# A spectral filter and a gated causal convolution on one core: filter loaded in fp32 through ScalarE's queue and converted on chip, sine tables with fewer passes and ordered ahead of what waits for the filter

## The chip, the core and the metric

The kernel runs on one core of a Trainium2 chip. The engines are PE (TensorE, matmuls; PEld is its weight load), DVE (VectorE), ACT (ScalarE), POOL (GpSimd) and SP (SyncE, which only issues DMAs here). Sixteen DMA engines move data between the chip's memory and the core's SBUF. The metric is the device time of one execution in microseconds (us), lower is better. The kernel before took 385.33 us, the median of 3 runs (384.27 to 386.5).

## What is computed

```python
def _attn_ref(x, filt_r, filt_i):            # x: (8, 3200, 256), filters: (1601, 256)
    X = np.fft.rfft(x, axis=1)
    F = (filt_r + 1j * filt_i)[None, :, :]
    return np.fft.irfft(X * F, n=x.shape[1], axis=1)

def _moe_ref(x, w_val, conv_w, w_out):       # x is the result above
    xp = np.concatenate([np.zeros((B, K - 1, D)), x], axis=1)      # K = 5
    for k in range(K):
        gate_pre += conv_w[k] * xp[:, k:k + S, :]
    gate = 1.0 / (1.0 + np.exp(-gate_pre))
    return gate * (x @ w_val) @ w_out
```
All inputs and the output are fp32. Each of the 8 batches has 3,200 positions of 256 channels.

## The kernel before

A Fourier transform of length 3,200 is done as two stages of small transforms, 3,200 = 128 x 25, each a matmul with a table of sines and cosines in fp16. A batch goes through these steps, each cut into seven chunks:

- `load_x` (L86, POOL's queue): x from memory, converted from fp32 to bf16 on the way. `xin` has 10 buffers, so three chunks of the next batch have room before the first seven are used.
- `s1` (first stage): PE multiplies with the matrix `cf_t` (L307), DVE evicts PSUM to the tile `so` (L310), and SP writes `so` to the scratch `dscr` in memory (L312). There are four PSUM tiles and four `so` buffers.
- `load_t` (SP): after all seven chunks are written, the scratch is read back in another order into the tiles `tt` (L326 to L329).
- `s2` (second stage): PE multiplies with `wc_t`, `ws_t`, `wsn_t` (L340 to L346), ACT evicts to `xs` (L349), and DVE multiplies with the filter: `za` with its real half `fr_t` (L354), `zb` with its signed imaginary half `fm_t` (L358), and their sum `z` (L360).
- `inva`: the inverse with `vc_t`, `vs_t`, `vsn_t` (L376, L378), evicted by ACT to `u` (L381) and written to the scratch `escr` (L392); `load_v` reads it back (L398).
- `invb` (L413 to L422), `conv` (L431, matrices `dg_t`, then the sigmoid on ACT), `val` (L448, L453), `outp` (L465 to L475): last inverse stage, causal convolution, gate and output.

A loop over 81 steps G runs all of these with lags: `s1` of chunk t at step t, `s2` at t + 9, `inva` at t + 10, `invb` at t + 19, `conv` at t + 21, `outp` at t + 23. So several batches are under way at once.

Before the loop stands a set-up, which the change is about. It builds the tables on the chip. An index product is made from iotas of POOL (`pcol`, `kc`, `kv`, `kt`, `nv`), reduced modulo the period by `floormod`, seven passes of DVE over the array (L103 to L113), and turned into a sine by ACT (L134, L182, L188). `expand` then spreads 25 columns of a group over five blocks with a mask `mk`, one multiply for each of 13 groups (L171), and `negate` makes the third table (L177). `sincos` does this for the `w` tables and again for the `v` tables. The filter is read by 24 DMAs on POOL's queue (L216 to L225) straight into bf16 tiles: twelve for each half, most of them 13 rows of 13 pieces or 12 rows of 13. DVE multiplies the imaginary half with a sign in each row, twice (L232, L234). Then come `ci_t` (L267) and the convolution's matrices `dg_t` (L284), twenty scalings on DVE.

A framework lays out each engine's instruction order: from text order as priority and from its own estimate of when things are ready. So the order on an engine is not the text's: `dg_t`, near the end of the set-up, has instructions among the first table passes. It also sets all waits, and the memory of the set-up's pools (`gen`, `gen2`, `genf`) is used again by pools opened after them. Each engine takes its instructions in the order laid out; issuing a DMA is an instruction of the engine that owns the queue.

## Time and profile before

| what | value | how to read it |
|---|---|---|
| median of 3 runs | 385.33 us | the time that is compared |
| the profiled execution | 387.95 us | one execution, the one that the profile shows |
| its span | 385.9 us | from the first to the last recorded instruction |
| PE / DVE / ACT / POOL busy | 312.3 / 284.9 / 229.1 / 64.2 us | whole span |
| DVE busy, 10 to 20 us | 9.97 us | the set-up's tables |
| hardware queue q1 | 78.98 MB, 62.5% | bytes, share of 16 engines' span |
| software queue q0 (POOL's) | 15.04 MB, 28.1% | the same; counted at bf16 |
| x loads 256 KB, issue to landing | 6.5 us | median over the run |
| half-filter pieces 78 KB, issue to landing | 6.2 us (real), 3.9 us (imaginary) | medians |

In the views, a row of the timeline has the start, the duration, engine, line, operation and tiles, and in brackets how long the engine sat idle before it and what it waited for. Busy shares count no instruction that only issues a DMA, save POOL's.

### The profile page before, as it was taken

What the parts mean: (1) busy time and instruction counts of PE and PEld (TensorE: products, weight loads), DVE (VectorE), ACT (ScalarE), POOL (GpSimd) and SP (SyncE); (2) the same over time, 40 slices, a digit from 0 to 9 for tenths busy, and PEclk for the clock granted to TensorE, in tenths of its full rate; (3) what the DMA queues carried; (4) which work ended last, traced back from release to release, by engine and by line L of the source; (5) the groups of instructions that cost most, each with busy time, mean ns of one, the idle gap of its engine ahead of it and who ended that gap; (6) DMA issues with size and microseconds to landing.
All of it is one profiled execution on the core that took longest, in us unless ns stands there. A gap on an engine that the chain in (4) does not pass through costs nothing.

```text
span 385.9 us, 8019 instructions
## 1 busy us (share of the span) xinstructions
PE 312.3 (81%) x3089; PEld 206.9 (54%) x3089; DVE 284.9 (74%) x462; ACT 229.1 (59%) x255; POOL 64.2 (17%) x131
## 2 busy tenths in 40 slices
PE   0230477475899999999997999899999999999992
PEld 0100145253656756766675666566676677666661
DVE  4999958553858887888787789678977677765554
ACT  1100235334976777677765776677677878867660
POOL 8797211112110211021102011100010001001000
PEclk9999998766989999999999999999999999999998
DMA  7999999999999999999999999989595968449343
GB/s 124 144 162 190 216 257 251 231 250 280 179 250 249 311 286 273 263 282 332 274 301 303 286 269 298 285 299 319 201 351 170 304 223 299 136 142 323 141 191 152
DMA packets 94118, 94.53 MB, mean 245 GB/s; under 512 B 10102, under 2 KB 74624, under 8 KB 94080
## 3 DMA queue, kind: packets, MB, share of 16 engines
q1 hardware_dynamic: 80064, 78.98, 62.5%
q0 software_dynamic: 14016, 15.04, 28.1%
q8 instruction: 24, 0.39, 0.4%
q14 instruction: 14, 0.11, 0.1%
HBM read 56.59 MB, written 52.43 MB: 282 GB/s over the span
## 4 chain that ended last, share of the span: by engine, by line
PE 44%; DVE 20%; DMA 19%; SPq 8%; issue 4%; ACT 2%; POOL 1%; DVEq 0%; ACTq 0%; POOLq 0%
PE ps L431 12%; PE ps L448 7%; DMA escr<-u 6%; PE ps L465 6%; DVE so L310 6%; DMA vt<-escr 5%; SPq L326 5%; PE ps L413 5%; DMA dscr<-so 4%; PE ps L376 3%; DVE gv L453 3%; DMA tt<-dscr 3%; PE ps L378 3%; PE ps L307 3%; DVE za L354 2%
## 5 line engine op out<-in xcount | busy, mean ns | idle before, releaser
L415 ACT ACTIVATE yt<-ps 128x1024 bf16<-128x1024 f32 (+1 forms) x56 | 52.1, 931 | 44.3 <-PE ps L413 44.2
L453 DVE TENSOR_TENSOR gv<-ps,gt 128x1024 bf16<-128x1024 f32 (+1 forms) x56 | 61.9, 1104 | 18.7 <-PE ps L448 13.7
L310 DVE CAST so<-ps 128x1024 bf16<-128x1024 f32 (+1 forms) x56 | 61.5, 1103 | 19.0 <-PE ps L307 15.9
L354 DVE TENSOR_TENSOR za<-xs,fr_t 125x1024 bf16<-125x1024 bf16 (+1 forms) x56 | 37.3, 665 | 50.5 <-ACT xs L349 50.3
L381 ACT ACTIVATE u<-ps 125x1024 bf16<-125x1024 f32 (+1 forms) x56 | 53.9, 963 | 24.4 <-PE ps L378 21.6
L431 PE MATMUL ps<-yt,dg_t 64*64 64x512 bf16 (+1 forms) x1120 | 65.7, 361 | 0.8
L349 ACT ACTIVATE xs<-ps 125x1024 bf16<-125x1024 f32 (+1 forms) x56 | 54.0, 965 | 19.6 <-PE ps L346 18.4
L436 ACT ACTIVATE gt<-ps 128x1024 bf16<-128x1024 f32 (+1 forms) x56 | 52.4, 935 | 9.1 <-PE ps L431 5.9
L86 POOL DMA_DIRECT2D xt<-in_x_dram x56 | 30.2, 569 | 153.0 <-PE ps L307 146.5
L307 PE MATMUL ps<-xt,cf_t 128*128 128x512 bf16 x112 | 36.9, 421 | 22.4 <-DVE so L310 11.4
L465 PE MATMUL ps<-wo_t,gv 128*128 128x256 bf16 x400 | 52.8, 273 | 0.9 <-DVE gv L453 0.9
L448 PE MATMUL ps<-yt,wv_t 128*128 128x512 bf16 (+1 forms) x224 | 52.6, 357 | 0.0
L465 PEld LDWEIGHTS <-gv 128*128 128x128 bf16 x400 | 39.1, 98 | 14.9 <-DVE gv L453 1.2
L413 PE MATMUL ps<-ci_t,vt 128*128 128x128 f16 x400 | 31.9, 221 | 13.3 <-DMA vt<-escr 9.6
L431 PEld LDWEIGHTS <-dg_t 64*64 64x64 bf16 x1120 | 30.1, 106 | 23.2 <-issue 10.1
L340 PE MATMUL ps<-tt,wc_t 125*128 125x256 bf16 x104 | 30.1, 289 | 12.9 <-DMA tt<-dscr 10.6
L470 DVE COPY o<-ps 128x1024 f32<-128x1024 f32 (+1 forms) x32 | 36.7, 1148 | 1.1 <-PE ps L465 1.1
L360 DVE TENSOR_TENSOR z<-za,zb 125x1024 bf16<-125x1024 bf16 (+1 forms) x56 | 36.4, 650 | 1.3
L413 PEld LDWEIGHTS <-vt 128*128 128x128 bf16 x400 | 27.0, 98 | 17.9 <-DMA vt<-escr 10.7
L358 DVE TENSOR_TENSOR zb<-xs,fm_t 125x1024 bf16<-125x1024 bf16 (+1 forms) x56 | 36.2, 646 | 0.0
L376 PE MATMUL ps<-z,vc_t 125*128 125x256 bf16 x104 | 30.0, 289 | 6.9 <-DVE z L360 6.9
L307 PEld LDWEIGHTS <-cf_t 128*128 128x128 f16 x112 | 9.2, 108 | 41.7 <-issue 28.2
(109 smaller groups left out, 386.6 us busy)
## 6 DMA issues: line engine op xcount, KB each, us to landing
out_dram<-o SPq DMA_DIRECT2D x32, 512.0 KB
tt<-dscr SPq DMA_DIRECT2D x48, 256.0 KB
escr<-u SPq DMA_DIRECT2D x48, 224.0 KB
out_dram<-o SPq DMA_DIRECT2D x24, 384.0 KB
xt<-in_x_dram POOLq DMA_DIRECT2D x32, 256.0 KB, 6.5
dscr<-so SPq DMA_DIRECT2D x32, 256.0 KB
vt<-escr SPq DMA_DIRECT2D x32, 256.0 KB
xt<-in_x_dram POOLq DMA_DIRECT2D x24, 192.0 KB, 5.7
```

Source lines behind the costliest of these rows:

```text
L307: nc.tensor.matmul(ps[:, a * D:e * D], lhsT=cf_t[:, 0:128], rhs=xt[:, a:e, :], start=True, stop=True)
L310: nc.vector.tensor_copy(so[:, 0:np_, :].rearrange("p a d -> p (a d)"), ps[:, 0:np_ * D])
L349: nc.scalar.activation(xs[0:P2, 0:ng, :, :].rearrange("p g c d -> p (g c d)"), ps[0:P2, 0:ng * 512], AF.Copy)
L354: nc.vector.tensor_tensor(za[0:P2, 0:ng], xs[0:P2, 0:ng], fr_t[0:P2, g0:g0 + ng, :].unsqueeze(2).to_broadcast((P2, ng, 2, D)), op=ALU.mult)
L381: nc.scalar.activation(u[0:P2, 0:2 * ng, :].rearrange("p q d -> p (q d)"), ps[0:P2, 0:ng * 512], AF.Copy)
L413: nc.tensor.matmul(ps[:, o:o + L], lhsT=v[:, a, 128 * dh:128 * dh + 128], rhs=ci_t[:, :], start=True, stop=True)
L415: nc.scalar.activation(y[:, :, H + p0:H + p0 + np_, :].rearrange("p h a n -> p h (a n)"), ps[:, :].rearrange("p (h n) -> p h n", h=2)[:, : ...
L431: nc.tensor.matmul(ps[64 * dh:64 * dh + 64, 512 * r:512 * r + np_ * L], lhsT=dg_t[rows, dh, k, :], rhs=y[rows, dh, p0 + k:p0 + k + np_, :] ...
L436: nc.scalar.activation(g[:, :, 0:np_ * L], ps[:, :].rearrange("p (h n) -> p h n", h=2)[:, :, 0:np_ * L], AF.Sigmoid)
L448: nc.tensor.matmul(ps[:, 512 * eh:512 * eh + np_ * L], lhsT=wv_t[:, dh, 128 * eh:128 * eh + 128], rhs=y[:, dh, H + p0:H + p0 + np_, :], st ...
L453: nc.vector.tensor_tensor(gv[:, :, 0:np_ * L], ps[:, :].rearrange("p (h n) -> p h n", h=2)[:, :, 0:np_ * L], g[:, :, 0:np_ * L], op=ALU.mult)
L465: nc.tensor.matmul(ps[:, D * a:D * a + D], lhsT=gv[:, eh, L * a:L * a + L], rhs=wo_t[:, eh, :], start=(eh == 0), stop=(eh == 1))
```

## The change

`s1` and `load_t` are defined ahead of the set-up, and batch 0's seven `s1` stand in the text right after `cf_t`; ACT instead of DVE evicts chunks 1, 3 and 5 of batch 0. The iotas `pcol` and `kc` come after the first x load instead of after the seventh. `floormod` is replaced: the product is scaled to turns, a large constant is added and taken away to round it, the rounded value is subtracted, and ACT takes the sine of the rest (three passes, one scaling ahead of them). `expand` becomes one multiply over all groups; `negate`, the two `fm_t` scalings and `dg_t` go to ACT. The filter is read in fp32 into `ff` by the same 24 pieces on ACT's queue, the real half's after ACT's eviction of chunk 1 and the imaginary half's after that of chunk 3 (`issue_after` lays them out behind the instruction named). DVE converts the real half after the last `v` table; ACT converts and signs the imaginary half. `zpool` and `upool` are opened before the set-up's pools. The small arrays `lp` and `rp` get new formulas, which the diff leaves out, as it does the unchanged parts of moved functions.

```diff
--- before.py
+++ after.py
@@ -65,13 +65,14 @@
     dg_t = cpool.tile([128, 2, K, 64], BF16, name="dg_t")
     wv_t = cpool.tile([128, 2, D], BF16, name="wv_t")
     wo_t = cpool.tile([128, 2, D], BF16, name="wo_t")
-    b_npi = cpool.tile([128, 1], FP32, name="b_npi")
 
     pp = ctx.enter_context(tc.tile_pool(name="ps", bufs=4, space=bass.MemoryType.PSUM))
     dpool = ctx.enter_context(tc.tile_pool(name="scr", bufs=2, space=bass.MemoryType.DRAM))
     xpool = ctx.enter_context(tc.tile_pool(name="xin", bufs=10))
     spool = ctx.enter_context(tc.tile_pool(name="s1o", bufs=4))
     tpool = ctx.enter_context(tc.tile_pool(name="s2i", bufs=8))
+    upool = ctx.enter_context(tc.tile_pool(name="ivo", bufs=4))
+    zpool = ctx.enter_context(tc.tile_pool(name="zed", bufs=3))
 
     def psum():
         return pp.tile([128, 1024], FP32, name="ps", tag="ps")
@@ -86,53 +87,85 @@
         nc.gpsimd.dma_start(out=xt[:, 0:np_, :], in_=src)
         xts[(b, j)] = xt
 
-    for j in range(NCH):
+    def iota(pool, shape, pattern, base, cm, name):
+        t = pool.tile(shape, FP32, name=name)
+        nc.gpsimd.iota(t[...], pattern=pattern, base=base, channel_multiplier=cm,
+                       allow_small_or_imprecise_dtypes=True)
+        return t
+
+    load_x(0, 0)
+    pcol = iota(cpool, [128, 1], [[0, 1]], 0, 1, "pcol")
+    kc = iota(cpool, [128, NG, 2, GL], [[5, NG], [0, 2], [1, GL]], 1, 0, "kc")
+    for j in range(1, NCH):
         load_x(0, j)
+
+
+    st = {}
+
+    def s1(b, j):
+        if j == 0:
+            st[("D", b)] = dpool.tile([128 * R + 64, D], BF16, name="dscr")
+        dscr = st[("D", b)]
+        p0, np_ = PCH[j]
+        xt = xts.pop((b, j))
+        ps = psum()
+        for a in range(0, np_, 2):
+            e = min(a + 2, np_)
+            nc.tensor.matmul(ps[:, a * D:e * D], lhsT=cf_t[:, 0:128],
+                             rhs=xt[:, a:e, :], start=True, stop=True)
+        so = spool.tile([128, 4, D], BF16, name="so")
+        sov = so[:, 0:np_, :].rearrange("p a d -> p (a d)")
+        if b == 0 and j % 2 == 1:
+            st[("Sact", j)] = nc.scalar.activation(sov, ps[:, 0:np_ * D], AF.Copy)
+        else:
+            nc.vector.tensor_copy(sov, ps[:, 0:np_ * D])
+        nc.sync.dma_start(
+            out=dscr[0:128 * R, :].rearrange("(i r) d -> i r d", r=R)[:, p0:p0 + np_, :],
+            in_=so[:, 0:np_, :])
+
+    def load_t(b, j):
...
+        st[("T", b, j)] = t
 
 
     with tc.tile_pool(name="gen", bufs=1) as g1, \
          tc.tile_pool(name="gen2", bufs=2) as g2, \
          tc.tile_pool(name="genf", bufs=1) as gf:
 
-        def floormod(src_ap, divisor):
-            shp = list(src_ap.shape)
...
-            return q
-
-        def iota(shape, pattern, base, cm, name):
-            t = g1.tile(shape, FP32, name=name)
-            nc.gpsimd.iota(t[...], pattern=pattern, base=base, channel_multiplier=cm,
-                           allow_small_or_imprecise_dtypes=True)
-            return t
-
-        nc.vector.memset(b_npi[:, :], -PI)
-        pcol = iota([128, 1], [[0, 1]], 0, 1, "pcol")
-
-
-        kc = iota([128, NG, 2, GL], [[5, NG], [0, 2], [1, GL]], 1, 0, "kc")
+        MAGIC = 1.5 * 2.0 ** 23
+
+        def sine(dst, t):
+
+            r = g2.tile(list(t.shape), FP32, name=f"sr{t.shape[1]}")
+            nc.vector.tensor_scalar(r[...], t, MAGIC, None, op0=ALU.add)
+            nc.vector.tensor_scalar(r[...], r[...], -MAGIC, None, op0=ALU.add)
+            nc.vector.tensor_tensor(r[...], t, r[...], op=ALU.subtract)
+            nc.scalar.activation(dst, r[...], AF.Sin, scale=2.0 * PI * (1.0 - 2e-7))
+
+
         nc.vector.memset(kc[:, NG - 1, 0, GL - 1:GL], 0.0)
         pr = g1.tile([128, NG, 2, GL], FP32, name="pr")
-        nc.vector.tensor_scalar(pr[...], kc[...], pcol[:, 0:1], None, op0=ALU.mult)
-        nc.vector.tensor_scalar(pr[:, :, 0, :], pr[:, :, 0, :], 0.75 * L, None,
-                                op0=ALU.add)
-        q = floormod(pr[...].rearrange("p g c l -> p (g c l)"), L)
-        nc.scalar.activation(cf_t[:, :], q[...], AF.Sin, bias=b_npi[:, 0:1],
-                             scale=2.0 * PI / L)
+        nc.vector.tensor_scalar(pr[...], kc[...], pcol[:, 0:1], 1.0 / L, op0=ALU.mult,
+                                op1=ALU.mult)
+        for c in range(2):
+            nc.vector.tensor_scalar(pr[:, :, c, :], pr[:, :, c, :], 0.25 * (c + 1), None,
+                                    op0=ALU.add)
+        sine(cf_t[:, :], pr[...].rearrange("p g c l -> p (g c l)"))
+
+        for j in range(NCH):
+            s1(0, j)
 
         ident = g1.tile([128, 128], FP32, name="ident")
         nc.vector.memset(ident[:, :], 1.0)
...
@@ -165,31 +200,32 @@
                                 channel_multiplier=-1)
         nc.vector.tensor_copy(mk[...], mkf[...])
 
-        def expand(dst, src):
+        def expand(eng, dst, src):
             nc.gpsimd.memset(dst[:, :, P2:128], 0.0)
-            for g in range(NG):
-                nc.vector.tensor_tensor(
-                    dst[:, g, 0:P2].rearrange("p (l r) -> p l r", l=GL),
-                    src[:, g, :].unsqueeze(1).to_broadcast((128, GL, R)),
-                    mk[...], op=ALU.mult)
+            return eng.tensor_tensor(
+                dst[:, :, 0:P2].rearrange("p g (l r) -> p g l r", l=GL),
+                src[...].unsqueeze(2).to_broadcast((128, NG, GL, R)),
+                mk[...].unsqueeze(1).to_broadcast((128, NG, GL, R)), op=ALU.mult)
 
         def negate(dst, src):
-            nc.vector.tensor_scalar(dst[...], src[...], -1.0, None, op0=ALU.mult)
-
-        def sincos(prod, dc, ds, dsn):
-            qs = floormod(prod[...].rearrange("p g r -> p (g r)"), N)
+            nc.scalar.activation(dst[...].rearrange("p g m -> p (g m)"),
+                                 src[...].rearrange("p g m -> p (g m)"),
+                                 AF.Copy, scale=-1.0)
+
+        def sincos(eng, prod, dc, ds, dsn):
             sn = g2.tile([128, NG, R], FP16, name="sn")
-            nc.scalar.activation(sn[...].rearrange("p g r -> p (g r)"), qs[...],
-                                 AF.Sin, bias=b_npi[:, 0:1], scale=2.0 * PI / N)
+            cs = g2.tile([128, NG, R], FP16, name="cs")
             pc = g2.tile([128, NG, R], FP32, name="pc")
-            nc.vector.tensor_scalar(pc[...], prod[...], 0.75 * N, None, op0=ALU.add)
-            qc = floormod(pc[...].rearrange("p g r -> p (g r)"), N)
-            cs = g2.tile([128, NG, R], FP16, name="cs")
-            nc.scalar.activation(cs[...].rearrange("p g r -> p (g r)"), qc[...],
-                                 AF.Sin, bias=b_npi[:, 0:1], scale=2.0 * PI / N)
-            expand(dc, cs)
-            expand(dsn, sn)
-            negate(ds, dsn)
+            flat = prod[...].rearrange("p g r -> p (g r)")
+            pcf = pc[...].rearrange("p g r -> p (g r)")
+            nc.vector.tensor_scalar(pcf, flat, 1.0 / N, 0.25, op0=ALU.mult, op1=ALU.add)
+            sine(cs[...].rearrange("p g r -> p (g r)"), pcf)
+            expand(eng, dc, cs)
+            nc.vector.tensor_scalar(flat, flat, 1.0 / N, None, op0=ALU.mult)
+            sine(sn[...].rearrange("p g r -> p (g r)"), flat)
+            last = expand(eng, ds, sn)
+            negate(dsn, ds)
+            return last
 
         HK = R // 2 + 1
         kv = g1.tile([128, NG, R], FP32, name="kv")
@@ -202,40 +238,40 @@
         nc.vector.tensor_scalar(kv[:, NG - 1, :], kv[:, NG - 1, :], lw[:, 0:1], None,
                                 op0=ALU.add)
         nc.vector.tensor_scalar(kv[...], kv[...], rp[:, 0:1], None, op0=ALU.mult)
-        sincos(kv, wc_t, ws_t, wsn_t)
-
-
-        fi_t = gf.tile([128, NG, D], BF16, name="fi_t")
+        sincos(nc.vector, kv, wc_t, ws_t, wsn_t)
+
+        for j in range(NCH):
+            load_t(0, j)
+
+
+        ff = gf.tile([128, 2, NG, D], FP32, name="ff")
 
         def fsrc(f, row, ap):
             return bass.AP(tensor=f.tensor, offset=f.offset + row * D, ap=ap + [[1, D]])
 
-        for f, dst in ((filt_r, fr_t), (filt_i, fi_t)):
+        def load_f(f, c):
+            dst = ff[:, c]
             for l in range(GL):
                 ng = NG if l < GL - 1 else NG - 1
-                nc.gpsimd.dma_start(
+                nc.scalar.dma_start(
                     out=dst[R * l:R * l + HK, 0:ng, :],
                     in_=fsrc(f, l + 1, [[L * D, HK], [GL * D, ng]]))
-                nc.gpsimd.dma_start(
+                nc.scalar.dma_start(
                     out=dst[R * l + HK:R * (l + 1), 0:ng, :],
                     in_=fsrc(f, L - l - 1, [[L * D, HK - 1], [-GL * D, ng]]))
             lo = R * (GL - 1)
-            nc.gpsimd.dma_start(out=dst[lo:lo + HK, NG - 1, :],
+            nc.scalar.dma_start(out=dst[lo:lo + HK, NG - 1, :],
                                 in_=fsrc(f, 0, [[L * D, HK]]))
-            nc.gpsimd.dma_start(out=dst[lo + HK:lo + R, NG - 1, :],
+            nc.scalar.dma_start(out=dst[lo + HK:lo + R, NG - 1, :],
                                 in_=fsrc(f, L, [[L * D, HK - 1]]))
-        sg = g1.tile([128, 1], FP32, name="sg")
-        sgn = g1.tile([128, 1], FP32, name="sgn")
-        nc.vector.tensor_scalar(sg[...], rp[...], HK - 0.5, None, op0=ALU.is_lt)
-        nc.vector.tensor_scalar(sg[...], sg[...], 2.0, -1.0, op0=ALU.mult, op1=ALU.add)
-        nc.vector.tensor_scalar(sgn[...], sg[...], -1.0, None, op0=ALU.mult)
-        nc.vector.tensor_scalar(fm_t[0:P2, :, 0, :], fi_t[0:P2, :, :], sgn[0:P2, 0:1],
-                                None, op0=ALU.mult)
-        nc.vector.tensor_scalar(fm_t[0:P2, :, 1, :], fi_t[0:P2, :, :], sg[0:P2, 0:1],
-                                None, op0=ALU.mult)
-
-
-        kt = iota([128, NG], [[5, NG]], 1, 0, "kt")
+
+        with tc.issue_after(st[("Sact", 1)].ins):
+            load_f(filt_r, 0)
+        with tc.issue_after(st[("Sact", 3)].ins):
+            load_f(filt_i, 1)
+
+
+        kt = iota(g1, [128, NG], [[5, NG]], 1, 0, "kt")
         nc.vector.tensor_scalar(kt[...], kt[...], lp[:, 0:1], None, op0=ALU.add)
         nc.vector.tensor_scalar(kt[:, NG - 1:NG], kt[:, NG - 1:NG], lw[:, 0:1], None,
                                 op0=ALU.add)
@@ -248,11 +284,24 @@
         nc.vector.tensor_tensor(rl[...], rl[...], rp[...], op=ALU.add)
         nc.vector.tensor_scalar(rl[...], rl[...], float(L), None, op0=ALU.mult)
         nc.vector.tensor_scalar(kt[...], kt[...], rl[:, 0:1], None, op0=ALU.add)
-        nv = iota([128, NG, R], [[0, NG], [1, R]], 0, 0, "nv")
+        nv = iota(g1, [128, NG, R], [[0, NG], [1, R]], 0, 0, "nv")
         nc.vector.tensor_tensor(nv[...], nv[...],
                                 kt[...].unsqueeze(2).to_broadcast((128, NG, R)),
                                 op=ALU.mult)
-        sincos(nv, vc_t, vs_t, vsn_t)
+        vs_ins = sincos(nc.vector, nv, vc_t, vs_t, vsn_t)
+
+
+        sg = g1.tile([128, 1], FP32, name="sg")
+        sgn = g1.tile([128, 1], FP32, name="sgn")
+        nc.vector.tensor_scalar(sg[...], rp[...], HK - 0.5, None, op0=ALU.is_lt)
+        nc.vector.tensor_scalar(sg[...], sg[...], 2.0, -1.0, op0=ALU.mult, op1=ALU.add)
+        nc.vector.tensor_scalar(sgn[...], sg[...], -1.0, None, op0=ALU.mult)
+        with tc.issue_after(vs_ins.ins):
+            nc.vector.tensor_copy(fr_t[0:P2, :, :], ff[0:P2, 0])
+        nc.scalar.activation(fm_t[0:P2, :, 0, :], ff[0:P2, 1], AF.Copy,
+                             scale=sgn[0:P2, 0:1])
+        nc.scalar.activation(fm_t[0:P2, :, 1, :], ff[0:P2, 1], AF.Copy,
+                             scale=sg[0:P2, 0:1])
 
 
         ac = g1.tile([128, 1], FP32, name="ac")
@@ -281,53 +330,15 @@
                                     in_=moe_w_out[ch:ch + 64, :])
                 for k in range(K):
                     rows = slice(64 * r, 64 * r + 64)
-                    nc.vector.tensor_scalar(dg_t[rows, dh, k, :],
-                                            ident[rows, 64 * r:64 * r + 64],
-                                            cw[rows, dh, k:k + 1], None, op0=ALU.mult)
-
-    zpool = ctx.enter_context(tc.tile_pool(name="zed", bufs=3))
-    upool = ctx.enter_context(tc.tile_pool(name="ivo", bufs=4))
+                    nc.scalar.activation(dg_t[rows, dh, k, :],
+                                         ident[rows, 64 * r:64 * r + 64], AF.Copy,
+                                         scale=cw[rows, dh, k:k + 1])
+
     vpool = ctx.enter_context(tc.tile_pool(name="ivi", bufs=8))
     ypool = ctx.enter_context(tc.tile_pool(name="yout", bufs=2))
     gpool = ctx.enter_context(tc.tile_pool(name="gate", bufs=3))
     opool = ctx.enter_context(tc.tile_pool(name="ost", bufs=4))
 
...
 
     def s2(b, j):
         g0, ng = GCH[j]
@@ -502,7 +513,7 @@
         if c is not None:
             conv(*c)
         c = at(G, 0)
-        if c is not None:
+        if c is not None and c[0] > 0:
             s1(*c)
             if c[1] == NCH - 1:
                 for j in range(NCH):
```

## The prediction

> **What bounds the kernel now.** I read the table of slices first: PE is under half busy for the first ten slices and nearly full afterwards, while DVE is full early. So the start differs from the rest. Then the windows, which put numbers on it, and the chain of waits, which says why.
>
> ```profile
> PE   0230477475899999999997999899999999999992
> DVE  4999958553858887888787789678977677765554
> ...
> 0.00:45.00 45.00, 8.33 (x19) 2.13 (x19) 38.35 (x157) 3.96 (x6) 34.13 (x70) 1.00 1.09 164
> 45.00:92.70 47.70, 29.52 (x165) 19.21 (x166) 30.76 (x43) 18.29 (x19) 5.59 (x12) 0.83 1.05 244
> 92.70:386.00 293.30, 274.46 (x2906) 185.61 (x2906) 215.74 (x263) 206.89 (x230) 24.44 (x49) 0.98 0.86 258
> ```
> The windows' columns are window, sum, then busy us of PE, PEld, DVE, ACT, POOL, then clock, DMA share, GB/s. After 92.7 us PE works 274 of 293 us: that part has the same code after the change. Before it PE works 37.9 of 92.7 us. The change can win only there.
>
> ```profile
> 10.07 0.40 ACT L134 ACTIVATE cf_t<-fm_q,b_npi 128x130 f16<-128x130 f32 x1 [7.98 <-DVE fm_q L113]
> ...
> PE ps L307 <- DVE so L310: 11.4, 3, 10.8
> ...
> 22.87 1.24 DVE so L310
> ...
> 31.03 3.13 DMA dscr<-so
> 34.60 1.70 SPq L326
> 37.03 4.30 SPq L326
> 41.37 5.33 SPq L326
> 46.75 4.58 SPq L326
> ...
> 45.09 0.37 PE L340 MATMUL ps<-tt,wc_t 125*128 125x256 bf16 x1 [4.11 <-DMA tt<-dscr]
> ```
> The first-stage matrix is ready at 10.5, and PE fills its PSUM tiles by 13.4; then it waits 10.8 us for the first eviction, which stands behind the sine tables on DVE until 22.87. The seven evictions end at 31.0, the write to scratch lands at 34.2, and the loads back take until 52.8 to issue, because batch 1's x loads are on the way at once. The first second-stage matmul runs at 45.1, the first product z ends at 51.2 (50.52 + 0.68), the last z of batch 0 at 73.2, and the first inverse matmul (L413) starts at 92.7. The filter is not in this chain: its landed halves are scaled at 33.2 to 37.0 (L232, L234), 11 us before they are used.
>
> **The change, part by part.**
>
> *x and the first matrix.* Only one x load (0.55 us) stands ahead of the two iotas (0.21 + 0.66), so kc is there at 1.31 + 0.55 + 0.87 = 2.7 instead of 6.0. Ahead of the Sin remain pr 0.55, two adds 0.22 each, three sine passes (0.26 + 0.26, and 0.28 as the nearest two-operand row): 1.8 us. With Sin 0.40, cf_t is ready at about 5, not 10.5. x is then late: the last of batch 0 is issued at 5.2 + 0.9 = 6.1 and takes 6.8 us to land, 12.9.
>
> *Evictions ahead of the tables.* Four on DVE (1.22 or 0.95), three on ACT (0.93 as L381 averages); after the last x a matmul pair (0.85) and one eviction, so the last `so` ends at about 15 against 31.0, its write lands (3.1) at 18 against 34.2: 16 us. The loads back took 11 us from first issue to first use (34.2 to 45.1), so 29 here, if they meet the same company.
>
> *Tables.* floormod's seven passes were 0.32 + 0.32 + 0.48 + 0.32 + 0.49 + 0.32 + 0.49 = 2.7 us for 325 columns; now a scaling and three passes, 0.32 x 3 + 0.49 = 1.45. Four times 1.3 is 5 us less DVE. The mask multiplies (13 x 0.14 pitch, 1.8 us) become one of 1,625 columns: between 0.95 (the rate of za, 706 ns for 1,024) and 1.8; I take 1.7, since broadcast operands resemble the old rows. Two negations (0.58) leave DVE for ACT, where the two Sin shapes give 0.84 ns a column (404 ns for 130, 568 for 325) on 0.295: 1.7 us each. Twenty dg_t scalings move too: 0.35 us each, 7.0; they are first read by L431 at 106.9, which covers them unless they stand ahead of the second stage's evictions, where they would cost their 7.0. DVE's saving buys nothing by itself, since evictions no longer wait for it.
>
> *Filter.* This becomes late next. Its 24 issues leave POOL, where they stood from 7.69 to 25.6 (17.9 us, 15.0 of it issuing); so batch 1's x loads start at about 31.8 - 17.9 = 13.9 and will share the DMA engines with filter, scratch write and loads back. On ACT they come behind evictions of chunks 1 and 3. An issue costs 0.46 us by the escr rows (median): 11 us. Three evictions and two Sin add 4, so from 10 the last is out at about 25 undisturbed. Data: 1.66 MB becomes 3.33 MB fp32, and the hardware queue spent 62.5% of the span on 78.98 MB, 3.05 us per MB: 10.2 us. The software queue spent 28.1% on 15.04 MB, 7.2 us per MB: the halves cost 12 there. That is even. Landing: at best 26 (25 and little company); at worst behind ten x loads, the buffers there are, 2.3 MB at the 205 GB/s of 8 to 12 us = 11.4 us, and the scratch traffic (3.3 MB, 10 us), 43. I take 33, in the middle, as all three queues get turns (in 40 to 48 us x had 89% and the loads back 24% of the engines' time).
>
> By the Trainium skill ("DMA: Bandwidth & Descriptors", section "Why a DMA increments its semaphore by 16 and not by 1") a transfer issued from this kind of queue spreads over the largest number of engines up to 16 that divides its slowest dimension; these pieces have 13 or 12 rows. No row of this trace shows it. It speaks against the change: an estimate by it is 10.2 x 16 / 12.5 = 13 us, and the forecast below would be 3 us less gain. I stay with the row.
>
> *Conversion.* fm_t on ACT: 2 x (0.295 + 3,328 x 0.84 ns) = 6.2 us (at the 1.0 ns of L349, 6.8), against 3.9 on DVE. fr_t on DVE, 2.0 us, runs beside it. Had the filter still been early, this would be free; now it is on the path. Two new waits come with it: fm_t waits for the filter on ACT, with dg_t and the second stage's evictions (L349) behind it, and fr_t on DVE, with batch 1's evictions and za behind it; SP carries none of the filter, and its loads back pass it by. So fm_t is ready at 39.2, and zb and z (0.69 each) end at 40.6 to 41, against 51.2: **-10 us**.
>
> *From there.* Batch 0's z came every (73.2 - 51.2) / 6 = 3.67 us. With everything landed DVE needs 2.07 for three passes and 1.1 for an eviction, 3.2: 6 x 0.47 = 2.8 us less; between 0 and 5, as the transfers must keep up. I take **-2**. The loads of batch 1, whose 5.0 us (75.7 to 80.7) stood in front of batch 0's last inverse, become due earlier alike. zpool and upool lie outside the set-up's memory now, so they wait for none of it: 0. Later batches: 0, covered by PE's 274 of 293 us.
>
> **Sum: -12 us.** The profiled execution took 387.95 (385.9 span, 2.05 around it), 2.6 above the median of 385.33. 387.95 - 12 - 2.6 = 373.3.
>
> **Rivals.**
> *Filter never late (chance 0.14).* It lands by 26, fm_t by 32, z is set by the loads back: 29, plus 6 as before (45.1 to 51.2), 35: -16, and up to -5 of pace: -21, 364. For: POOL is free and the filter has a queue of its own. Against: ten x loads wait in the same engines.
> *Transfers set the start anyway (0.20).* The DMA share is 1.05 to 1.09 up to 92.7 already; 18 to 22 us alone shows clear idleness (0.86 and 0.49). If x hogs, the filter lands at 43 and z ends at 51, as before: 0 to -6, with -3 likely: 382. About a third of this lies within 0.5%, which is what a measurement of this kernel can tell from no change.
> *ACT's queue blocks (0.14, the other side).* The loads back needed a median of 3.0 us each to issue while x loads were under way (34 to 52 us), against 0.50 over the run: the queue stops when the engines are behind. The filter pieces have a third of their rows (169 against 512), so 1.0 us each: 24 us. If evictions of chunks 3 and 5 stand behind all 24, they wait until 10.6 + 24 = 34.6, the last `so` ends at 35.5, and every later step is 35.5 - 31.0 = 4.5 us late: 390. It decides once the last eviction of batch 0 ends after 31.0. For: nothing in the trace passes a waiting instruction on its engine (the evictions' 10.8 us), and the scheduler fills gaps out of text order (dg_t, written near the end, at 7.62). Against: evictions precede the loads in the text, and x is there by 13.
> *The passes do little:* whether DVE's setup shrinks at all doesn't matter for the sum; the order does.
>
> **How the numbers follow.** Forecast (-7 to -17, 368 to 378): 0.52. Beyond it: 0.14. Transfers: 0.20, a third of it "same". Blocked: 0.14, nearly all slower. Faster 0.52 + 0.14 + 0.14 = 0.80, same 0.07, slower 0.13. The range leaves out the blocked case and little else: 363 to 384.
>
> **What would show it.** Right: first `so` before 10 us and last by 17; batch 1's x loads from about 14; first z near 41, held by fm_t on ACT; the L413 start near 80. Wrong: filter issues of 1 us and more on ACT ahead of its evictions of chunks 3 and 5; first z after 48; xs waiting on ACT behind dg_t; or an L413 start that moves while the end doesn't, which would say that the later batches are not PE's but the transfers'.

## The result, and the profile after

| | before | after |
|---|---|---|
| median | 385.91 us (384.27 to 386.5, 4 runs) | 410.53 us (409.52 to 418.22, 4 runs) |
| after / before | | 1.0642, 95% interval 1.0597 to 1.0688 |
| profiled execution, span | 387.95, 385.9 us | 418.22, 416.5 us |
| first conversion of the filter (fm_t) starts | 33.2 us | 70.8 us |
| first z ends | 51.2 us | 84.4 us |
| first yt, ScalarE's first piece of the gated part | 93.7 us | 123.7 us |
| span behind the first yt | 292.2 us | 292.8 us |

The change makes the kernel 24.6 us slower; 373.3 was predicted. The profiled execution was a disturbed one, 7.7 us above the median, so the delay of its start is read here as some 7 us too long, and the times of the experiments are compared by their medians; the profiled executions of h and i were disturbed ones too (393.72 and 402.93 us, against 386.02 and 392.9 at their fastest).

The slices of the changed kernel, 40 of 10.4 us each:

```profile
PE   2313100075639899997999799989999999999993
DVE  5841003178537788788578767977888777765564
...
DMA  7999985049999999999999999989969689548344
GB/s 111 227 226 239 234 122 73 0 94 199 265 252 208 255 244 309 270 294 251 331 264 305 242 328 268 319 251 325 307 225 317 197 257 299 187 144 288 151 195 164
```

PE now starts earlier (2 and 3 in the first two slices, 0 and 2 before), does next to nothing in the fifth and stands idle from the sixth to the eighth. In that gap even the DMA engines end up idle. The windows, with the columns as before, cut at 71 and 123.7:

```profile
0.00:45.00 45.00, 13.82 (x39) 4.44 (x39) 21.64 (x61) 7.86 (x13) 19.96 (x48) 1.00 1.06 207
45.00:71.00 26.00, 0.00 (x0) 0.00 (x0) 3.78 (x3) 2.30 (x8) 0.00 (x0) 1.00 0.81 135
71.00:123.70 52.70, 23.89 (x151) 16.68 (x154) 26.32 (x38) 27.79 (x32) 4.50 (x10) 0.85 0.66 153
123.70:416.50 292.80, 270.82 (x2863) 184.33 (x2896) 215.63 (x263) 207.04 (x230) 24.34 (x49) 0.98 0.87 257
```

The last window has before's length and before's work. DVE does 21.6 us in the first 45 instead of 38.4, as the change intends. But from 45 to 71 us PE does nothing, DVE and ScalarE work for 3.78 and 2.30 us, and the transfers run on at 135 GB/s. ScalarE's timeline says what is awaited:

```profile
4.56 0.31 ACT L155 ACTIVATE cf_t<-sr 128x130 f16<-128x130 f32 x1 [2.47 <-DVE sr L154]
...
16.77 0.32 ACTq L259 DMA_DIRECT2D ff<-in_filt_r_dram  x1
...
25.19 0.31 ACTq L256 DMA_DIRECT2D ff<-in_filt_r_dram  x1
32.29 0.30 ACTq L259 DMA_DIRECT2D ff<-in_filt_r_dram  x1
44.02 0.36 ACTq L256 DMA_DIRECT2D ff<-in_filt_r_dram  x1
...
63.16 0.32 ACTq L265 DMA_DIRECT2D ff<-in_filt_i_dram  x1
63.53 0.48 ACT L155 ACTIVATE cs<-sr 128x325 f16<-128x325 f32 x1 [40.59 <-DMA ff<-in_filt_i_dram]
...
70.83 3.07 ACT L301 ACTIVATE fm_t<-ff,sgn 125x3328 bf16<-125x3328 f32 x1 [5.15 <-DMA ff<-in_filt_i_dram]
73.80 1.57 ACT L211 ACTIVATE vsn_t<-vs_t 128x1664 f16<-128x1664 f16 x1
75.28 3.05 ACT L303 ACTIVATE fm_t<-ff,sg 125x3328 bf16<-125x3328 f32 x1
78.24 2.58 ACT L333 ACTIVATE dg_t<-ident,cw 64x64 bf16<-64x64 f32 x10
80.84 1.94 ACT L360 ACTIVATE xs<-ps 125x1024 bf16<-125x1024 f32 x2
```

cf_t is ready at 4.9 (10.5 before). The pieces of the filter don't issue slowly, at 0.3 us each; they wait. The fifth of 24 leaves at 44.0, the last at 63.2. Behind the last stand the Sins of the v tables, which waited 40.6 us for nothing but their place in the queue, and then the conversions, a negation, ten dg_t and the first xs.

The chain of waits says what a piece waits for. The eighth leaves at 46.06, when a scratch write of batch 1, from SP's queue, has landed; from there on pieces wait for pieces:

```profile
40.99 5.05 DMA dscr<-so
46.06 8.89 DMA ff<-in_filt_r_dram
54.97 8.17 DMA ff<-in_filt_i_dram
63.16 7.35 DMA ff<-in_filt_i_dram
```

In the chains of kernels c and i (below) it is one of batch 0's loads back that lets the fifth piece go (7.00 us from 35.94 in c, 5.27 from 27.81 in i). So a piece on ScalarE's queue stands behind transfers of SP's.

Two readings of the DMA queues give the rest (queue, packets, MB, share of 16 engines' time). From 28 to 36 us:

```profile
q0 software_dynamic: 801, 1.35, 90.3%
q1 hardware_dynamic: 496, 0.25, 14.9%
q10 hardware_dynamic: 183, 0.17, 7.7%
```

q0 is POOL's queue, which holds nothing but x of batches 1 and 2 now (L87 issues it from 16.84 on); q1 is SP's, q10 ScalarE's. The filter moves 0.17 MB in 8 us, about one piece: the third left at 25.19, the fourth at 32.29, and it offers no more. And from 52 to 64 us, when the filter is alone:

```profile
DMA packets 1569, 1.47 MB, mean 122 GB/s; under 512 B 137, under 2 KB 1569, under 8 KB 1569
...
q10 hardware_dynamic: 1569, 1.47, 86.9%
```

It occupies the engines to 87% and gets 122 GB/s out of them, 8.2 us per MB. Kernel f below, with the same rows and source, gets 158 GB/s, 6.3 us per MB. The step of the loads back is late too, and it lies among the same transfers. SP's queue:

```profile
8.41 11.29 SPq L122 DMA_DIRECT2D dscr<-so  x7
27.23 11.29 SPq L136 DMA_DIRECT2D tt<-dscr  x6
```

The six loads of L136 take 11.3 us to issue, and the first second-stage matmul (L351) runs at 37.45, before the filter's fifth piece has been issued.

### The profile page after: what moved, and what is told of

Same layout as the page of the kernel before. It is cut to its first block, busy times and chain, and to the rows that moved or that the text cites. A ratio compares the mean times of both kernels' runs of the same rounds, so it can differ in the third digit from the quotient of the medians.

```text
span 416.5 us, 7912 instructions
## 1 busy us (share of the span) xinstructions
PE 308.5 (74%) x3052; PEld 205.5 (49%) x3089; DVE 267.4 (64%) x365; ACT 245.0 (59%) x282; POOL 48.8 (12%) x107
## 3 DMA queue, kind: packets, MB, share of 16 engines
q0 software_dynamic: 9472, 13.37, 22.1%
q10 hardware_dynamic: 3550, 3.33, 4.8%
## 4 chain that ended last, share of the span: by engine, by line
PE 45%; DMA 26%; DVE 14%; SPq 5%; ACT 4%; issue 4%; POOL 0%; ACTq 0%; DVEq 0%; POOLq 0%
PE ps L442 11%; DMA dscr<-so 8%; PE ps L459 7%; PE ps L476 6%; DVE so L121 5%; DMA escr<-u 5%; PE ps L424 5%; DMA vt<-escr 4%; DMA ff<-in_filt_i_dram 4%; PE ps L387 4%; PE ps L389 3%; SPq L136 3%; DVE gv L464 2%; PE ps L114 2%; DMA ff<-in_filt_r_dram 2%
## 5 line engine op out<-in xcount | busy, mean ns | idle before, releaser
L121 DVE CAST so<-ps 128x1024 bf16<-128x1024 f32 (+1 forms) x53 | 58.7, 1108 | 37.6 <-PE ps L114 21.4
L365 DVE TENSOR_TENSOR za<-xs,fr_t 125x1024 bf16<-125x1024 bf16 (+1 forms) x56 | 37.3, 665 | 63.2 <-ACT xs L360 63.1
L459 PE MATMUL ps<-yt,wv_t 128*128 128x512 bf16 (+1 forms) x208 | 51.7, 355 | 0.9
L87 POOL DMA_DIRECT2D xt<-in_x_dram x56 | 29.9, 538 | 161.7 <-PE ps L114 76.4
L114 PE MATMUL ps<-xt,cf_t 128*128 128x512 bf16 x91 | 32.0, 419 | 18.0 <-DMA xt<-in_x_dram 17.8
L351 PE MATMUL ps<-tt,wc_t 125*128 125x256 bf16 x104 | 30.2, 290 | 16.2 <-DMA tt<-dscr 13.9
L387 PEld LDWEIGHTS <-vc_t 125*128 125x128 f16 x104 | 10.4, 100 | 60.2 <-issue 46.5
L424 PEld LDWEIGHTS <-vt 128*128 128x128 bf16 x400 | 27.3, 99 | 21.6 <-issue 12.2
```

The lines of the kernel that those rows point to most:

```text
L114: nc.tensor.matmul(ps[:, a * D:e * D], lhsT=cf_t[:, 0:128], rhs=xt[:, a:e, :], start=True, stop=True)
L121: nc.vector.tensor_copy(sov, ps[:, 0:np_ * D])
L387: nc.tensor.matmul(ps[:, oh:oh + D], lhsT=t0[0:P2, g, :], rhs=z[0:P2, a, 0, :], start=True, stop=False)
L424: nc.tensor.matmul(ps[:, o:o + L], lhsT=v[:, a, 128 * dh:128 * dh + 128], rhs=ci_t[:, :], start=True, stop=True)
L459: nc.tensor.matmul(ps[:, 512 * eh:512 * eh + np_ * L], lhsT=wv_t[:, dh, 128 * eh:128 * eh + 128], rhs=y[:, dh, H + p0:H + p0 + np_, :], st ...
```

## Experiments

Twelve kernels. The first four ran together beside before at 385.58 us, the next four beside 384.44, three beside 384.15 and the last beside 385.58.

**a. The filter part undone.** The 24 pieces go through POOL's queue again, cast to bf16 into fr_t and fi_t, and DVE scales them.

```diff
-        ff = gf.tile([128, 2, NG, D], FP32, name="ff")
+        fi_t = gf.tile([128, NG, D], BF16, name="fi_t")
...
-                nc.scalar.dma_start(
+                nc.gpsimd.dma_start(
...
-        nc.scalar.activation(fm_t[0:P2, :, 0, :], ff[0:P2, 1], AF.Copy, scale=sgn[0:P2, 0:1])
+        nc.vector.tensor_scalar(fm_t[0:P2, :, 0, :], fi_t[0:P2, :, :], sgn[0:P2, 0:1], None, op0=ALU.mult)
```

> The changed kernel with only the filter part undone: 24 pieces on POOL's queue, converted to bf16 on the way, fm_t on DVE, no conversion of fr_t; fast tables, early first stage, ACT's dg_t and negations stay. Theory 1 (the filter's new way alone costs the time; the order and the tables win): first z of batch 0 before 45 us, against 51 before and 84 after the change, and 370 to 380 us in all. Rival (the order itself costs, since batch 1's x or ACT's extra work get in the way): 386 us or more.

Measured: 381.27 us (378.73 to 385.25), 0.9867 of before (0.9796 to 0.9939). Its windows:

```profile
0.00:45.00 45.00, 11.67 (x33) 3.84 (x34) 26.52 (x64) 15.72 (x32) 33.67 (x71) 1.00 1.09 186
45.00:87.80 42.80, 25.31 (x162) 17.32 (x161) 27.81 (x40) 17.07 (x19) 5.44 (x12) 0.82 1.06 256
87.80:380.50 292.70, 273.78 (x2898) 185.36 (x2896) 215.39 (x263) 207.06 (x230) 24.34 (x49) 0.98 0.87 257
```

First yt at 87.8, and again 292.7 us behind it. So the filter part costs about 29 us (410.5 against 381.3), and the rest of the change gains some 4, less than expected: 381.27 lies just past 370 to 380, and the first z ends at 48.2, not before 45. In its chain stands x of batch 1, issued at 35.85 behind 24 pieces and eight weight loads on POOL; g and k ask whether that is what holds it.

**b. The filter part alone, in the kernel before.** The same pieces on ScalarE's queue, with before's order and tables, and no wait for an eviction ahead of them.

```diff
-                nc.gpsimd.dma_start(
+                nc.scalar.dma_start(
...
+        nc.vector.tensor_copy(fr_t[0:P2, :, :], ff[0:P2, 0])
```

> The kernel before with only the filter part of the change: fp32 pieces on ACT's queue, free to start at once, fr_t converted by DVE and fm_t by ACT. Theory 1a (the fp32 pieces need some 28 us of transfer whenever they start: 3.33 MB at the 118 GB/s of the stretch in which they were alone): issued from 1 us on, they land by 35 to 42 us, fm_t is ready by 50, first z 50 to 55, 385 to 392 us in all. Theory 1b (what hurts is that they start late, behind waits shared with SP's transfers; the transfer itself takes 10 to 15 us): landed by 20 to 25 us, first z no later than before, 384 to 387. Rival (a DMA on ACT's queue holds ACT however early): first z after 60, over 395.

Measured: 415.42 us, 1.0760 (1.0687 to 1.0834). Both forms of the first theory fell; the rival's numbers came (first z at 84.9). On ScalarE's timeline the first piece leaves at 0.81 us, and still:

```profile
20.54 0.30 ACTq L219 DMA_DIRECT2D ff<-in_filt_r_dram  x1
40.46 0.31 ACTq L216 DMA_DIRECT2D ff<-in_filt_r_dram  x1
49.58 0.30 ACTq L219 DMA_DIRECT2D ff<-in_filt_r_dram  x1
...
66.61 0.32 ACTq L225 DMA_DIRECT2D ff<-in_filt_i_dram  x1
66.97 0.57 ACT L182 ACTIVATE sn<-fm_q,b_npi 128x325 f16<-128x325 f32 x1 [50.46 <-DMA ff<-in_filt_i_dram]
```

Starting early doesn't help, so the place of the loads behind the evictions is not the reason.

**c. Rows apart.** Each piece goes into every tenth row instead of 12 or 13 neighbouring ones; same bytes, source and order. The products then read other rows of the filter.

```diff
-                    out=dst[R * l:R * l + HK, 0:ng, :],
+                    out=dst[l:l + 10 * (HK - 1) + 1:10, 0:ng, :],
```

> The changed kernel, but each piece of the filter lands in every tenth SBUF row instead of in 13 or 12 neighbouring rows; bytes, sizes, source, order and waits are the same (the filter's rows are then permuted, so the products use other rows). Theory R (neighbouring rows limit the write): in the stretch where the pieces are alone they move over 200 GB/s instead of 118, the last lands before 62 us instead of 70, and the run is 6 to 14 us shorter than the changed kernel, some 397 to 404. Theory S (the source's stride of 128 KB limits) and theory E (12 or 13 of 16 engines limit): 118 GB/s as before, 410 us.

Measured: 406.07 us, 1.0532 (1.045 to 1.0614), 4.5 us faster than the changed kernel where 6 to 14 were expected, with intervals that just overlap. The fifth piece still leaves at 42.95, but then the pieces follow each other, an issue now taking 0.81 to 0.87 us, and the first conversion starts at 62.3. The queues from 46 to 58 us:

```profile
DMA packets 2483, 2.40 MB, mean 200 GB/s; under 512 B 212, under 2 KB 2466, under 8 KB 2483
q10 hardware_dynamic: 2329, 2.19, 58.6%
```

A packet costs 0.586 x 16 x 12 us / 2,329 = 48 ns of an engine, against 0.869 x 16 x 12 / 1,569 = 106 ns in the changed kernel and 0.866 x 16 x 10 / 1,693 = 82 ns in f, at the same 0.94 KB. So where the rows lie sets the filter's own rate. The number of rows of a piece, 13 or 12, is the same here, so it is not what holds the rate down. The Trainium skill ("SBUF — State Buffer", section "Door 1: The DMA port swizzle") says that a transfer's rate depends on how many of 16 ports its partitions reach, that partitions 0 to 15 reach four, and gives 104 GB/s measured and 109 at best for that. Here the pieces alone, several on the way at once, moved 122 GB/s in the changed kernel and 158 in f, more than the page gives for one transfer, and 200 were moved with rows apart; the direction agrees, the figure does not. No run here shows the ports themselves.

**d. Source rows adjacent.** The other side of the same transfer; other rows of the filter are read.

```diff
-                    in_=fsrc(f, l + 1, [[L * D, HK], [GL * D, ng]]))
+                    in_=fsrc(f, 160 * l, [[D, HK], [HK * D, ng]]))
```

> The changed kernel, but each piece of the filter reads rows that lie next to one another in memory instead of 128 KB and 5 KB apart; bytes, sizes, destination, order and waits are the same (other rows of the filter are read). Theory S (the source's stride limits): the stretch where the pieces are alone moves 200 GB/s or more and the run is 6 to 14 us shorter, some 397 to 404. Theories R and E: 118 GB/s there as before, 410 us.

Measured: 413.33 us, 1.0721 (1.0635 to 1.0806): no gain, and the first conversion at 68.8. Alone on the engines the pieces moved 134 to 150 GB/s. f, with the changed kernel's source, moved 158 GB/s, so no cost of the stride shows, and it is not what sets the time.

**e. Scratch traffic of batch 0 on POOL's queue.** The aim was to leave SP next to nothing that a piece on ScalarE's queue could wait for; the loads back are changed in the same way, and POOL's set-up stands ahead of stage 1 in the text.

```diff
-        nc.sync.dma_start(
+        q = nc.gpsimd if b == 0 else nc.sync
+        q.dma_start(
             out=dscr[0:128 * R, :].rearrange("(i r) d -> i r d", r=R)[:, p0:p0 + np_, :],
             in_=so[:, 0:np_, :])
```

> The changed kernel with batch 0's scratch writes and loads back on POOL's queue, so that SP issues only the two small conv-weight loads before batch 1; the filter pieces stay fp32 on ACT's queue. POOL's set-up instructions stand ahead of stage 1 in the text, so that they don't wait behind the writes. Nothing is left out. Theory Q (a piece on ACT's queue waits until a DMA eight places earlier of SP's and ACT's queues taken together has landed, so the late loads back of SP hold pieces 3 to 5 until 25, 32 and 44 us): without SP's DMAs among them pieces 2 to 4 are issued by 24 us, behind wsn_t, the fifth follows within 8 us, the last is issued by 52 and landed by 55; first z at 62 to 70, time 388 to 397. Rival (the pieces wait for each other only, or for the memory): the last piece is issued at 60 or later and the time stays at 405 or above.

Measured: 411.07 us (406.36 to 412.68). The theory's first half came true, and its end did not:

```profile
22.70 0.92 ACTq L261 DMA_DIRECT2D ff<-in_filt_r_dram  x1
33.52 0.31 ACTq L258 DMA_DIRECT2D ff<-in_filt_r_dram  x1
35.60 0.30 ACTq L261 DMA_DIRECT2D ff<-in_filt_r_dram  x1
35.95 0.40 ACTq L258 DMA_DIRECT2D ff<-in_filt_r_dram  x1
47.11 0.30 ACTq L261 DMA_DIRECT2D ff<-in_filt_r_dram  x1
```

Six pieces are out by 22.7, where the changed kernel had two. Then they wait again, and the last leaves at 60.1, as the rival said. But the rival's reason, that pieces wait for each other only, is not what the chain shows:

```profile
40.71 8.16 DMA dscr<-so
48.89 0.32 ACTq L267
```

The twelfth piece leaves when a scratch write of SP's has landed. The edit moved batch 0's scratch only; SP writes batch 1's from 27.72 on. By the trace's completion records four of these writes land at 33.5, 35.6, 47.1 and 48.9, just when the seventh, eighth, tenth and twelfth piece leave. So the wait on SP's transfers was not taken away here, it passed from batch 0's to batch 1's, and this kernel doesn't say what the filter would do without it.

**f. Conversion, negation and dg_t back on DVE**, the filter still fp32 on ScalarE's queue.

```diff
-        nc.scalar.activation(fm_t[0:P2, :, 0, :], ff[0:P2, 1], AF.Copy, scale=sgn[0:P2, 0:1])
+        nc.vector.tensor_scalar(fm_t[0:P2, :, 0, :], ff[0:P2, 1], sgn[0:P2, 0:1], None, op0=ALU.mult)
```

> The changed kernel with the conversions to fm_t, the negations and the conv diagonals on DVE, as before; the filter stays fp32 on ACT's queue. Theory: the landing of the last piece (70.8 us) stays, and what stood on ACT between it and the first xs (fm_t 3.07 and 3.05, vsn_t 1.47, ten dg_t 2.6: 10 us) goes, but DVE has two conversions of some 2 us each more ahead of the first product; so the first z comes 4 to 8 us earlier and the time is 402 to 407. Rival (the work on ACT is what makes it late, the pieces only stand between): below 395. Rival (DVE is as late): 409 to 412.

Measured: 408.78 us (405.35 to 409.72), 1.0619 (1.0564 to 1.0674), just slower than expected and 1.8 us faster than the changed kernel (0.9 by the ratios), with intervals that overlap. The two conversions take 3.68 and 3.67 us on DVE, on the path, instead of some 2. Work moved to ScalarE is a small part of the loss. The queues from 51 to 61 us, with the filter alone:

```profile
DMA packets 1693, 1.58 MB, mean 158 GB/s; under 512 B 147, under 2 KB 1693, under 8 KB 1693
q10 hardware_dynamic: 1693, 1.58, 86.6%
```

**g. x of batch 1 ahead of the filter**, in kernel a.

```diff
+        for j in range(3):
+            load_x(1, j)
...
         fi_t = gf.tile([128, NG, D], BF16, name="fi_t")
```

> The kernel with only the filter part undone, with the first three x loads of batch 1 and the two iotas of the v table put ahead of the filter's pieces on POOL's queue. Theory (in that kernel PE's second stage stands in order behind batch 1's first chunks, and these wait for x, which waits behind 24 filter pieces, the weights and their issue): x of batch 1 is there by 14 us, stage 1 of it no longer waits, the filter lands some 4 us later (fm_t at 37 to 39), first z at 43 to 46, time 374 to 379. Rival (the filter's landing sets the start as much): first z at 48 or later and 380 to 384.

Measured: 385.86 us, 1.0030 (1.0002 to 1.0057): 374 to 379 was wrong, and so was the rival's 380 to 384. The first z ended at 47.2 (48.2 in a), but fm_t's first half started at 41.4 (34.6), and the other four chunks of batch 1 came behind everything, from 43.6 on. In its chain batch 1's scratch write takes 10.6 us from 59.98, and the first yt stands at 91.8. Moving one load forward moved another back by as much.

**h. The fp32 pieces on POOL's queue.** Same bytes, rows and conversions as the changed kernel; the loads no longer stand behind evictions of ScalarE.

```diff
-                nc.scalar.dma_start(
+                nc.gpsimd.dma_start(
...
-        with tc.issue_after(st[("Sact", 1)].ins):
-            load_f(filt_r, 0)
-        with tc.issue_after(st[("Sact", 3)].ins):
-            load_f(filt_i, 1)
+        load_f(filt_r, 0)
+        load_f(filt_i, 1)
```

> The changed kernel with the fp32 pieces issued from POOL's queue and not ACT's; same bytes, same destination, same conversions on ACT. If the queue is what cost (theory Q with ACT's order): pieces issued from 8 to 28 us, last landed at 36 to 43 by the 118 GB/s that the lone pieces of the changed kernel show, first z 50 to 55, time 380 to 388. If the doubled bytes are what cost: landed after 50, first z after 60, above 393. This separates the change's first half (fp32) from its second (ACT's queue).

Measured: 1.0106 of before (1.0053 to 1.0159), 388.5 us by that ratio; the median over nine runs is 391.95, a ratio of 1.0195. The last piece is issued at 30.7, the first conversion starts at 41.3, the first z ends at 56.0. Expected was 380 to 388 and a first z at 50 to 55, so both lie past the upper end. The queues from 12 to 28 us:

```profile
q0 software_dynamic: 1244, 2.54, 70.1%
q1 hardware_dynamic: 1003, 1.63, 35.0%
```

POOL's queue, with the filter and the end of batch 0's x, moves 2.04 KB per packet on average at 0.701 x 16 x 16 / 1,244 = 144 ns, 71 ns per KB against 113 in the changed kernel and 88 in f. The filter goes there in half as many packets for the same bytes, and takes its turn ahead of batch 1's x. So of the 7.8 points between kernel a and the changed one (0.9867 to 1.0642), fp32 with its conversions accounts for 2.4 (9 us), and ScalarE's queue for 5.4 (21 us); by the median over nine runs it is 3.3 and 4.5 (13 and 17 us).

**i. x held.** In the changed kernel, x of batch 1 from its third chunk on waits on POOL until the first conversion has run.

```diff
...
+            if c == (1, 2):
+                hold = nc.gpsimd.tensor_copy(gate_t[0:P2, :], fm_t[0:P2, NG - 1, 0, 0:1])
+            if c[0] == 1 and c[1] >= 2:
+                with tc.issue_after(hold.ins):
+                    load_x(*c)
+            else:
+                load_x(*c)
```

> The changed kernel with batch 1's x loads, from its third chunk on, held on POOL's queue until the first conversion of the filter has run on ACT. Nothing is left out. Theory P (from 12 to 44 us the DMA engines are full, and POOL's queue, which no longer carries the filter, fills them with batch 1's x, which is not needed yet): without these five loads the loads back of batch 0 land by 35, the fifth piece is issued by 36 (44.0), and the first conversion starts at 58 to 64 (70.8). Since x then comes later to batch 1, the gain in time is smaller than that: 400 to 406. Theory R alone (the pieces write neighbouring rows at 118 GB/s, whatever else runs): 24 pieces take their 28 us after the fifth has been issued in any case, so the same start of the conversion as the fifth piece gives; it differs from P only if the fifth is not earlier. Rival (x is no hindrance): first conversion at 69 or later.

Measured: 402.82 us (402.93, 402.82 and 392.9). On ScalarE's timeline the fifth piece leaves 11 us earlier, and the conversion starts 14 us earlier, 12 against kernel d:

```profile
31.83 0.30 ACTq L260 DMA_DIRECT2D ff<-in_filt_r_dram  x1
33.10 0.31 ACTq L257 DMA_DIRECT2D ff<-in_filt_r_dram  x1
...
56.84 3.07 ACT L302 ACTIVATE fm_t<-ff,sgn 125x3328 bf16<-125x3328 f32 x1 [4.62 <-DMA ff<-in_filt_i_dram]
```

SP's queue in the same run, with the six loads back at 3.1 us instead of 11.3:

```profile
25.75 3.12 SPq L137 DMA_DIRECT2D tt<-dscr  x6
```

The theory held, the conversion even a little before its range. The size of the gain stays uncertain by these three runs, which lie 10 us apart. x, loaded for later, is what the loads back and the filter stood behind.

**l. Both: scratch on POOL's queue and x held.** The edits of e and i together.

```diff
+        q = nc.gpsimd if b == 0 else nc.sync
...
+                with tc.issue_after(hold.ins):
+                    load_x(*c)
```

> The kernel with batch 0's scratch traffic on POOL's queue, and batch 1's x loads held as in the run beside it: both suspects taken away, so that ACT's pieces wait only for their own predecessors and share the engines only with the scratch. If the two together explain the late filter: pieces are issued in one stream from 21 us on, the first conversion starts at 48 to 55 (66.1 with the scratch alone moved), first z at 60 to 67, time 388 to 397. If the pieces' own rate is lower than 118 GB/s would give even then: first conversion after 58, time above 400.

Measured: 398.89 us, 1.0391 (1.0334 to 1.0449). Eight pieces are out by 24.5, but the ninth waits until 38.2, and the first conversion starts at 57.9, not 48 to 55. With x held, moving the scratch as well makes the filter no earlier; the time is lower than i's median by 3.9 us, within i's spread. This expectation fell, and the other one (over 400 us) was not met either. As in e, SP's queue was not out of the way: in the chain the tenth piece, at 39.55, stands behind a scratch write of batch 1 that takes 10.63 us from 28.90.

Against e, its partner without the hold, l's first conversion starts 8.2 us earlier and its time is 12.2 us lower.

**m. x held and rows apart.** The edits of c and i together; the products read other rows.

```diff
+                with tc.issue_after(hold.ins):
+                    load_x(*c)
...
+                    out=dst[l:l + 10 * (HK - 1) + 1:10, 0:ng, :],
```

> The changed kernel with batch 1's x held from its third chunk on, and each piece put into every tenth row as in the run with rows apart (same bytes; the products read other rows). If the two causes stand one behind the other and add: the fifth piece is issued at 32 to 34 us, the remaining twenty at their issue time of 0.8 us each, the first conversion starts at 49 to 53 (56.8 with x held alone, 62.3 with rows apart alone, 70.8 with neither), the time is 394 to 400. If holding x has already taken what the rows gave: first conversion at 56 or later, 401 to 404.

Measured: 393.30 us (393.2 to 394.58), 1.0219 (1.0132 to 1.0307), just under the range. The fifth piece leaves at 31.6, and the first conversion lies within its range of 49 to 53:

```profile
47.98 0.79 ACTq L266 DMA_DIRECT2D ff<-in_filt_i_dram  x1
50.98 3.07 ACT L302 ACTIVATE fm_t<-ff,sgn 125x3328 bf16<-125x3328 f32 x1
```

The pieces now follow each other at the pace of their issue. By the medians the two gains add and more: 410.5, 406.1 (c), 402.8 (i), 393.3 with both. That is shown for holding x: against c, which differs from m only by the hold, it gives 12.8 us. It is not shown for the rows: against i they give 9.5 us by the median, but i's third run, 392.9, was as fast as m, and only the first conversion (51.0 against 56.8) speaks for them. Both together bring back 17.2 us, about as much as ScalarE's queue cost by h (17 to 21).

**k. The weights last**, in kernel a: the eight loads of wv_t and wo_t behind batch 1's x, as a search for a faster version.

```diff
-                nc.gpsimd.dma_start(out=wo_t[64 * dh:64 * dh + 64, r, :],
-                                    in_=moe_w_out[ch:ch + 64, :])
...
+        if G == NCH:
+            load_w()
```

> The kernel with only the filter part undone (381.27 us beside 385.58 for before), with the eight loads of wv_t and wo_t moved behind batch 1's x on POOL's queue. Theory (batch 1's x, which PE's stage 1 waits for ahead of the second stage of batch 0, stands behind 24 pieces and eight weight loads of 0.5 to 0.8 us each): x of batch 1 is issued from 28 to 30 us (35.8), the first xs comes 2 to 5 us earlier, time 376 to 380. Rival (the filter's landing and the inverse stage set the first yt whatever x does): 380 to 383. A third (the weights then hold batch 2's x): slower than 383.

Measured: 382.08 us (12 runs), 0.9920 (0.9883 to 0.9956). x is issued from 28.8 (35.8) and the first xs starts at 40.5 (43.8), as expected, but the first za stays where it was, 45.3 against 45.7, and so does the time. The rival's numbers came; so x's place behind the weights was not what set a's start. Kernels a and k are both about 1% faster than before; their intervals overlap.

Over all of them the end follows the first yt, 286.8 to 294.3 us behind it; differences smaller than this spread of 7.5 us can't be put down to the start by this table alone (us):

| kernel | first conversion | first yt | span | span behind it |
|---|---|---|---|---|
| before | 33.2 | 93.7 | 385.9 | 292.2 |
| after | 70.8 | 123.7 | 416.5 | 292.8 |
| k | 35.2 | 86.5 | 379.2 | 292.7 |
| a | 34.6 | 87.8 | 380.5 | 292.7 |
| g | 41.4 | 91.8 | 384.4 | 292.6 |
| h | 41.3 | 97.7 | 392.0 | 294.3 |
| m | 51.0 | 103.8 | 391.6 | 287.8 |
| i | 56.8 | 109.2 | 401.2 | 292.0 |
| l | 57.9 | 110.4 | 397.2 | 286.8 |
| c | 62.3 | 112.9 | 404.2 | 291.3 |
| f | 66.6 | 115.2 | 403.6 | 288.4 |
| e | 66.1 | 118.3 | 407.8 | 289.5 |
| d | 68.8 | 121.5 | 412.3 | 290.8 |
| b | 75.2 | 123.3 | 413.2 | 289.9 |

## Why the prediction was wrong

*What bounds the kernel* was read rightly. The later batches change by nothing (292.2 and 292.8 us), and every kernel's end follows its start to within 7.5 us.

*x and the first matrix:* cf_t at 4.9, about 5 predicted. Right.

*Evictions ahead of the tables:* the first starts at 7.2, the last ends at 19.4 rather than 15. The sum left out that there are only four `so` buffers: ScalarE waited 4.4 us and DVE 1.3 for scratch writes to land. The loads back were first used at 37.45, not 29. "If they meet the same company" was the condition, and they met worse: with x held, SP issued them in 3.1 us (i).

*Tables and negation:* a mask multiply takes 1.03 us (1.7), so the bound from za's rate was the right one; a negation 1.59 (1.7), a conversion 3.07 and 3.05 (6.2 in all). Right or better, and worth little, as was said.

*Filter:* this is the step that failed, in the sentence "Landing: ... I take 33, in the middle, as all three queues get turns", whose worst case was 43. It landed just before 70.8 (66.6 in f). Three of its terms were wrong.
- "the last is out at about 25 undisturbed" added up issue times of 0.46 us. They were right (0.30 to 0.62), but pieces also wait for transfers to land, and not only for those of their own queue: "SP carries none of the filter, and its loads back pass it by" left that wait at nothing. The fifth piece left behind loads back (c, i) and the eighth behind batch 1's scratch write, at 46.06, and the last at 63.2. Moving batch 0's scratch to POOL (e) did not end the waits on SP, so what they cost alone stays open.
- "All three queues get turns": the filter's queue got 7.7% of the engines' time while x on POOL's had 90.3%. That x would start at about 14 and share the engines stood in the prediction; holding it gives 7.7 us in the median of i, 12.2 from e to l and 12.8 from c to m. The step saw the neighbour and priced it as if turns were equal. The small share is not all a matter of turns: a piece that waits offers nothing.
- "3.05 us per MB: 10.2 us" was the average of a whole queue. The filter's own packets of 0.94 KB into neighbouring rows took 8.2 us per MB, so 27 us for 3.33 MB; at f's 6.3 it is 21. The 13 us estimated beside it by the rule on the number of engines would have been short as well; no run shows that split, and in c pieces of the same 13 or 12 rows went at 48 ns per packet. Rows apart alone give 4.5 us by the medians (c).

*Conversion:* from landing to the end of the first z were 8 us predicted and 13.6 measured. vsn_t (1.57), ten dg_t (2.58) and an xs (1.03) stood between. The prediction had named the case in which dg_t stands ahead of the second stage, and left it out of the sum. f puts its worth at 1 to 2 us.

*From there:* from the first za to the first yt 45.6 us before, 41.8 after: -3.7 for -2, within its bounds.

*The sum:* even with the filter as it was, the rest gives 4 us (a). x of batch 1, behind filter and weights on POOL, is in a's chain, but moving it forward (k, g) gains nothing. In g the filter and batch 1's scratch are late in its place; what holds the start in k was not shown.

*The rivals:* "ACT's queue blocks" had the right side but not this mechanism: no eviction of batch 0 waited behind a piece, the last ended at 19.4, before its own point of 31.0. What waited were the v tables, the conversions and xs. "Transfers set the start" named x rightly, with the filter at 43 as its worst. "Filter never late" was wrong by more than 40 us.

*Left open:* kernel m's fifth piece still leaves at 31.6, where kernel h has issued its last at 30.7. How much of the rest, 393.3 against 388.5 to 392.0, is waits and how much is the longer issue of rows apart was not tried. No kernel takes all of SP's transfers out of the way of the pieces. Nor was x held for good: it only comes later.

## What to carry to other kernels

A transfer that moves to another queue leaves its old queue free, and what stood behind it there now runs first; price the transfer against that traffic, at the share of the engines its queue gets, not at equal turns. Ask of each DMA what it waits for before it is issued: here pieces on one queue stood behind transfers of another. Take its rate from rows of its own shape, with the same packet size and the same few rows, because a queue's average was off by two to nearly three times here (3.05 us per MB against 6.3 and 8.2). And a load that waits in an engine's queue holds everything behind it, however cheap its issue is: 40 us here for two Sins of half a microsecond.
